# Attention steps that load their inputs first in a turn instead of last, with the squares at the turn's end

## The chip, the cores and the metric

One core of a Trainium2 chip runs the whole program. Its engines are PE (TensorE, matmuls), DVE (VectorE), ACT (ScalarE), POOL (GpSimd) and SP (SyncE, which here only issues DMAs, one after the other in program order). The metric is the device time of one execution in microseconds; lower is better. The kernel before takes 2015.22 us as the median of three runs.

## What is computed

The reference cut to what matters: an attention with random features, a mixture of eight experts on its result, and a second feed-forward stage.

```
q_s, k_s = (q * scale, k * scale)                 # (4, 8, 576, 64)
def phi(x):
    proj = einsum('bhsd,md->bhsm', x, omega)      # 128 features
    sq = sum(x * x, axis=-1, keepdims=True) / 2.0
    h = proj - sq
    h = h - max(h, axis=-1, keepdims=True)
    return exp(h) / sqrt(m)
q_p, k_p = (phi(q_s), phi(k_s))
kv = einsum('bhsm,bhsd->bhmd', k_p, v)
z = sum(k_p, axis=2)
num / den = q_p against kv and z
...
for e in range(E): out += P[:, e:e+1] * (maximum(x @ w1[e], 0.0) @ w2[e])
...
h = maximum(maximum(x @ w1, x @ w2), x @ w3);  return h @ w_out
```

The change touches the attention alone: the row sums of squares (`sq`), and the order of the loads around them.

## The kernel before

The attention has 16 steps, one for each batch and pair of heads. A step's keys and queries come as two tiles: `raw` (features on the partitions, for the matmuls; three buffers) and `sq` (tokens on the partitions, for the row sums of squares; two buffers), 576 KB each, loaded by SP in `load`. POOL squares `sq` in place (`squares`), DVE sums it to `bias` (`norms`), PE projects `raw` with `om` in three portions of 4, 4 and 1 token tiles (`A`), DVE takes the maxima of each portion and turns sums and maxima into a bias, and ACT makes the exponentials (`exps`, "E" in the list), `kp` for the first portion, `qp` for the second, `rem` for the last. `KV`, `QT`, `num` ("N") and `X` of earlier steps fill the rest: the products with the values, the transposes of `qp`, the quotient (ending in `xs`), and the transpose of the quotient into `xf`.

The program is a loop over turns from -2 on. The list `ORDER` says in which order a turn's pieces are written: `("A", 0, 0, 4)` is piece A of the step that belongs to this turn, a lag of -1 means the next turn's step, -2 the one after it. The instructions of each engine run in exactly this written order. `J` takes one job from a list that is there from time to time: in turns 5 to 13 the splits of finished `xf` blocks into `xh`, `xl` and differences `t` on POOL, and from turn 13 on the preparation of the first expert weights (`s`, `wh`, `wl` out of the loaded `st`), whose first four jobs are DVE additions. `G` is the expert logits, in turns 6, 10, 14 and 18 only.

From step 8 on (second half of the tokens) `X` also writes its block to DRAM: a DMA `x_of<-xf` on SP's queue that waits for ACT's copy in that turn, one for each of X's two parts. These turns are 10 and later. In turn 13 the first weight load `st` follows the second of these. Feed-forward layers begin in turn 16, and then take the rest of the span.

The first two steps are loaded ahead of the loop (`START`), and step 0's squares are made in two portions there.

Of the kernel before, what the change touches and what calls it, by code (L numbers as in the profile page):

```python
# [43 lines left out]
}  # L44

ORDER = [
# [3 lines left out]
]  # L50


# [1 line left out]
def tile_performer__moe__max3(ctx, tc, kq_t, kq, v1, omega2, w_gate, w1, w2, m1, m2, m3, m_out, out):  # L54
# [12 lines left out]
    N, DM = out.shape  # L67
    S = N // B
    E, _, FF = w1.shape
# [6 lines left out]
    G = HALF // S  # L76
# [33 lines left out]
    def tt(on, out, in0, in1, op):  # L110
        (nc.gpsimd if on == "P" else nc.vector).tensor_tensor(out=out, in0=in0, in1=in1, op=op)  # L111
# [457 lines left out]
    def attention(pool, proj_pool):  # L569
# [36 lines left out]
        def parts(s):  # L606
            return (slice(0, 4), slice(4, TP)) if s == 0 else (slice(0, TP),)
# [26 lines left out]
        def norms(s, part=None):  # L634

            if not part:
                bias[s] = proj_pool.tile([P, 2, TP, 2], F32, tag="bias", name="bias", bufs=2)
            bt = bias[s]
            for t in parts(s) if part is None else parts(s)[part : part + 1]:
                n = sq[s][:, t]  # L640
                if s == 0:
                    nc.scalar.square(n, n) if t.start else tt("P", n, n, n, ALU.mult)
                nc.vector.tensor_reduce(out=bt[:, 0, t], in_=n, axis=AX.X, op=ALU.add)
# [175 lines left out]
        def job():  # L819
            while todo:  # L820
# [4 lines left out]
                j()  # L825
                return True

        stages = dict(
            load=load, v=load_v, squares=squares, norms=norms,
            A=A, E=exps, KV=KV, QT=QT, N=num, X=X, G=logits,  # L830
        )
        early = {("squares", 0)}
# [3 lines left out]
        for turn in range(-2, NS + 3):  # L836
# [5 lines left out]
            for f, lag, *more in ORDER:  # L842
                s = turn - lag
# [44 lines left out]
    with tc.manual_schedule():  # L888
        make_identity(nc, ident)

        left = tc.tile_pool(name="att", bufs=1, side="left")
        right = tc.tile_pool(name="proj", bufs=1, side="right")
        with left as att:
            with right as proj:
                steps = attention(att, proj)
                while next(steps) < B * HP:
                    pass
            pools["a"] = ctx.enter_context(tc.tile_pool(name="a", bufs=1, side="right"))
            wslot[1] = tuple(pools["a"].tile([P, 7, 2, P], F32R, name=f"w{c}1") for c in "hl")
            load_ahead(2)  # L900
            layers = feed_forward()
            for n, _ in enumerate(steps):
                if n < FILL:
                    next(layers)
        smalls.clear()
        pools["b"] = ctx.enter_context(tc.tile_pool(name="b", bufs=1, side="left"))
        acc = big.tile([P, HT, DM], F32, tag="acc", name="acc")
        extra = gate()
        for n, _ in enumerate(layers):
            if n % 3 == 0:  # L910
                next(extra, None)
# [56 lines left out]
```

## Time and profile before

| | before |
|---|---|
| median of three runs | 2015.22 us (2014.66 to 2016.46) |
| the profiled execution | 2013.28 us, of it the span 2011.5 us |
| PE busy | 1955.9 us, 97% of the span |
| DVE, ACT, POOL busy | 1412.2, 805.9, 719.8 us |
| chain that ended last, by engine | PE 90%, DVE 5%, ACT 2%, DMA 1% |
| one line of that chain | DMA sq<-in_kq_dram 1% |

The busy shares are averages over a span of which the attention's turns 0 to 15 take the first 160 us or so. The chain of waits is followed back from the last instruction; a DMA in it is a transfer for which everything that came after it had to wait.

### The profile page before, as it was taken

The numbers are of one execution on the slowest core, as the hardware profiler recorded it, in microseconds if no ns is written. First come the engines' busy times: TensorE is split into PE (matmuls) and PEld (weight loads), VectorE is DVE, ScalarE is ACT, GpSimd is POOL, SyncE is SP. The second block draws the span as 40 slices with busy tenths as digits, with TensorE's granted clock in tenths as the row PEclk, the third lists the DMA queues.
The fourth block names the chain that finished last, engine by engine and source line by source line (L and its number), as shares of the span: only waits on it lengthen the run. The fifth ranks groups of instructions, "written<-read, shape, count | busy, mean of one in ns | idle before, by whom it ended". The sixth has DMA issues, their size and how long they took to land.

```text
span 2011.5 us, 33572 instructions
## 1 busy us (share of the span) xinstructions
PE 1955.9 (97%) x12906; PEld 1757.2 (87%) x12906; DVE 1412.2 (70%) x2735; ACT 805.9 (40%) x2011; POOL 719.8 (36%) x583
## 2 busy tenths in 40 slices
PE   7979999999999999999999999999999998998999
PEld 6868888998999889988899998999999897997898
DVE  6855778788878887768666666666666668658755
ACT  6865333333333333335333333333333334443442
POOL 3742234444443444324332222333322224333530
PEclk9989999999999999999999999999999999999999
DMA  6452112222222222223111111111111122212201
GB/s 207 166 162 77 43 48 74 91 84 84 74 74 74 74 79 94 63 74 93 62 47 49 43 43 43 43 43 53 52 44 43 43 66 71 85 43 90 90 22 48
DMA packets 93921, 143.42 MB, mean 71 GB/s; under 512 B 6848, under 2 KB 49984, under 8 KB 93760
## 3 DMA queue, kind: packets, MB, share of 16 engines
q1 hardware_dynamic: 93760, 141.28, 21.6%
q8 instruction: 101, 1.65, 0.3%
q14 instruction: 60, 0.49, 0.1%
HBM read 123.17 MB, written 18.09 MB: 70 GB/s over the span
## 4 chain that ended last, share of the span: by engine, by line
PE 90%; DVE 5%; ACT 2%; DMA 1%; issue 1%; POOL 0%; SPq 0%; DVEq 0%; ACTq 0%; POOLq 0%
PE ph L116 15%; PE ph L117 14%; PE ph L118 14%; PE po L394 9%; PE po L393 9%; PE po L395 9%; PE small L394 5%; PE small L393 5%; PE small L395 5%; PE ph L663 1%; PE ph L597 1%; DMA sq<-in_kq_dram 1%; DVE s L111 1%; DVE xl L111 1%; ACT qp L686 1%
## 5 line engine op out<-in xcount | busy, mean ns | idle before, releaser
L116 PE MATMUL ph<-xh,wh 128*128 128x288 f32 x2296 | 686.2, 299 | 17.1 <-ACT u L375 6.1
L117 PE MATMUL ph<-xl,wh 128*128 128x288 f32 x2296 | 681.3, 297 | 3.5 <-DVE xl L111 3.5
L118 PE MATMUL ph<-xh,wl 128*128 128x288 f32 x2296 | 677.6, 295 | 0.0
L116 PEld LDWEIGHTS ph<-xh,wh 128*128 128x128 f32 x2296 | 432.7, 188 | 51.1 <-ACT u L375 9.6
L117 PEld LDWEIGHTS ph<-xl,wh 128*128 128x128 f32 x2296 | 433.3, 189 | 29.2 <-DVE xl L111 4.2
L118 PEld LDWEIGHTS ph<-xh,wl 128*128 128x128 f32 x2296 | 434.2, 189 | 0.0
L411 DVE SCALAR_TENSOR_TENSOR acc<-po,prob,acc 128x512 f32<-128x512 f32 x354 | 265.3, 749 | 239.0 <-PE po L395 237.2
L111 POOL TENSOR_TENSOR w2l<-st,w2h 128x512 fp32r<-128x512 f32 x140 | 185.7, 1349 | 626.8 <-ACT w2h L108 600.8
L337 ACT ACTIVATE h<-ph 128x288 fp32r<-128x288 f32 x384 | 157.9, 412 | 451.4 <-DVE ph L111 402.0
L394 PE MATMUL po<-w2l,h 128*128 128x512 f32 x836 | 330.5, 395 | 0.0
L395 PE MATMUL po<-w2h,h 128*128 128x512 f32 x836 | 329.1, 394 | 0.4 <-DVE h L346 0.4
L393 PE MATMUL po<-w2h,h 128*128 128x512 f32 x836 | 329.5, 394 | 0.0
L111 POOL TENSOR_TENSOR wl<-st,wh 128x512 fp32r<-128x512 f32 (+1 forms) x162 | 169.4, 1052 | 281.6 <-ACT wh L108 280.4
L111 POOL TENSOR_TENSOR wl<-s,wh 128x512 fp32r<-128x512 f32 x162 | 214.6, 1329 | 33.1 <-ACT wh L108 29.7
L411 DVE SCALAR_TENSOR_TENSOR acc<-small,prob,acc 128x512 f32<-128x512 f32 x177 | 132.3, 748 | 84.9 <-PE small L395 84.6
L395 PEld LDWEIGHTS po<-w2h,h 128*128 128x128 f32 x836 | 157.7, 189 | 36.9 <-DVE h L346 0.8
L111 DVE TENSOR_TENSOR ph<-ph,u 128x288 f32<-128x288 f32 x304 | 140.1, 461 | 67.1 <-PE ph L118 53.8
L393 PEld LDWEIGHTS po<-w2h,h 128*128 128x128 f32 x836 | 157.7, 189 | 19.2
L394 PEld LDWEIGHTS po<-w2l,h 128*128 128x128 f32 x836 | 157.7, 189 | 18.4
L338 DVE SCALAR_TENSOR_TENSOR h<-ph,h 128x288 fp32r<-128x288 f32 x384 | 171.4, 447 | 1.2 <-ACT h L337 0.6
L394 PE MATMUL small<-w2l,h 128*128 128x512 f32 x424 | 167.2, 394 | 0.0
L395 PE MATMUL small<-w2h,h 128*128 128x512 f32 x424 | 166.3, 392 | 0.2 <-DVE h L346 0.2
(165 smaller groups left out, 2444.0 us busy)
## 6 DMA issues: line engine op xcount, KB each, us to landing
st<-in_moe_w_dram SPq DMA_DIRECT2D x146, 512.0 KB, 3.7
st<-plain SPq DMA_DIRECT2D x24, 512.0 KB, 3.7
raw<-in_kq_t_dram SPq DMA_DIRECT2D x15, 576.0 KB, 4.8
sq<-in_kq_dram SPq DMA_DIRECT2D x15, 576.0 KB, 6.0
plain<-d SPq DMA_DIRECT2D x24, 256.0 KB, 2.3
x_of<-xt SPq DMA_DIRECT2D x18, 256.0 KB, 2.7
out_dram<-acc SPq DMA_DIRECT2D x18, 256.0 KB, 2.0
v<-in_v_dram SPq DMA_DIRECT2D x16, 260.0 KB, 2.8
```

What stands on the lines that cost most here:

```text
L111: (nc.gpsimd if on == "P" else nc.vector).tensor_tensor(out=out, in0=in0, in1=in1, op=op)
L116: nc.tensor.matmul(ps, wh, xh, start=start and not onto, stop=False, **given)
L117: nc.tensor.matmul(ps, wh, xl, start=False, stop=False, **given)
L118: nc.tensor.matmul(ps, wl, xh, start=False, stop=stop, **given)
L337: after(0, lambda: nc.scalar.activation(hh, c, AF.Relu))
L338: after(1, lambda: nc.vector.scalar_tensor_tensor(out=hl, in0=c, scalar=0.0, in1=hh.bitcast(F32), op0=ALU.max, op1=ALU.subtract))
L393: nc.tensor.matmul(ps, h[:, f, ts], wh[:, f], start=f == 0, stop=False)
L394: nc.tensor.matmul(ps, h[:, f, ts], wl[:, f], start=False, stop=False)
L395: nc.tensor.matmul(ps, h[:, 2 + f, ts], wh[:, f], start=False, stop=f == 1)
L411: nc.vector.scalar_tensor_tensor(out=a, in0=ps, scalar=prob[:, i, e : e + 1], in1=a, op0=ALU.mult, op1=ALU.add)
L597: nc.tensor.matmul(o[j], w[:, j], x, start=start, stop=stop)
L663: nc.tensor.matmul(ps[h][:, i], x[d, t0 + i], om[d, h * M : (h + 1) * M], start=True, stop=True)
```

## The change

The load of the step two turns ahead moves from near the end of a turn to its very start. The squares move from the start of the turn before their step to the end of the turn two before it, behind N and ahead of the last J. The sum of squares (`norms`) stays where it is, right behind the first E, for all steps but step 1: that step's sum moves from the middle of turn 0 to its end (`late`).

```
 ORDER = [
-    ("squares", -1), ("A", 0, 0, 4), ("QT", 1, 0), ("X", 2, 1), ("QT", 1, 2), ("QT", 1, 1), ("G", 3), ("E", 0, 0, 4),
+    ("load", -2), ("A", 0, 0, 4), ("QT", 1, 0), ("X", 2, 1), ("QT", 1, 2), ("QT", 1, 1), ("G", 3), ("E", 0, 0, 4),
     ("v", 0), ("norms", -1), ("J", 0), ("A", 0, 4, 4), ("KV", 1), ("J", 0), ("X", 2, 0), ("E", 0, 4, 4),
-    ("A", 0, 8, 1), ("E", 0, 8, 1), ("N", 1), ("load", -2), ("J", 0),
+    ("A", 0, 8, 1), ("E", 0, 8, 1), ("N", 1), ("late", -1),
+    ("squares", -2), ("J", 0),
 ]
...
-            load=load, v=load_v, squares=squares, norms=norms,
+            load=load, v=load_v, squares=squares,
+            norms=lambda s, *part: s == 1 or norms(s, *part), late=lambda s: s == 1 and norms(s),
```

PE and ACT have the same rows in the same order in both kernels. Three engines' orders change.

On SP, around turns 9 to 11 before the change (`raw_1533`, `sq_1534` are step 11, `raw_1708`, `sq_1709` step 12, `v1_122` and `v0_121` the values of steps 9, 10 and 11 in turn):

```order
L624 DMA v1_122<-in_v1_dram 128x520
L625 DMA v1_122<-in_v1_dram 64x130
L613 DMA raw_1533<-in_kq_t_dram 128x1152
L614 DMA sq_1534<-in_kq_dram 128x1152
L764 DMA x_of1_96<-xf11_120 128x64
L624 DMA v0_121<-in_v1_dram 128x520
L625 DMA v0_121<-in_v1_dram 64x130
L764 DMA x_of1_96<-xf10_119 128x512
L613 DMA raw_1708<-in_kq_t_dram 128x1152
L614 DMA sq_1709<-in_kq_dram 128x1152
```

The same place after it (`raw_1392` and `sq_1393` are step 11, `raw_1540` and `sq_1541` step 12, `raw_1715` and `sq_1716` step 13):

```order
L614 DMA raw_1392<-in_kq_t_dram 128x1152
L615 DMA sq_1393<-in_kq_dram 128x1152
L625 DMA v1_122<-in_v1_dram 128x520
L626 DMA v1_122<-in_v1_dram 64x130
L614 DMA raw_1540<-in_kq_t_dram 128x1152
L615 DMA sq_1541<-in_kq_dram 128x1152
L765 DMA x_of1_96<-xf11_120 128x64
L625 DMA v0_121<-in_v1_dram 128x520
L626 DMA v0_121<-in_v1_dram 64x130
L765 DMA x_of1_96<-xf10_119 128x512
L614 DMA raw_1715<-in_kq_t_dram 128x1152
L615 DMA sq_1716<-in_kq_dram 128x1152
```

Step 12's two loads stood behind both DRAM writes of turn 10, and now stand ahead of them; step 13's stand behind them, where step 12's were.

On DVE, turn 0 before the change, from the bias of its first portion on (`bias<-sq 128x18` is the sum of squares of step 1, the reductions out of `po` and `ph` with 128x4 are the maxima, those with 128x2 the maxima of the last token tile):

```order
L680 SCALAR_TENSOR_TENSOR bias<-bias,small 128x8
L643 TENSOR_REDUCE bias<-sq 128x18
L666 TENSOR_REDUCE small<-po 128x4
L666 TENSOR_REDUCE small<-ph 128x4
L677 SCALAR_TENSOR_TENSOR small<-bias,small 128x8
L680 SCALAR_TENSOR_TENSOR bias<-bias,small 128x8
L657 TENSOR_REDUCE small<-ph 128x2
L677 SCALAR_TENSOR_TENSOR small<-bias,small 128x2
L680 SCALAR_TENSOR_TENSOR bias<-bias,small 128x2
L838 MEMSET gate_w 128x128
```

And after it:

```order
L681 SCALAR_TENSOR_TENSOR bias<-bias,small 128x8
L667 TENSOR_REDUCE small<-po 128x4
L667 TENSOR_REDUCE small<-ph 128x4
L678 SCALAR_TENSOR_TENSOR small<-bias,small 128x8
L681 SCALAR_TENSOR_TENSOR bias<-bias,small 128x8
L658 TENSOR_REDUCE small<-ph 128x2
L678 SCALAR_TENSOR_TENSOR small<-bias,small 128x2
L681 SCALAR_TENSOR_TENSOR bias<-bias,small 128x2
L644 TENSOR_REDUCE bias<-sq 128x18
L841 MEMSET gate_w 128x128
```

The sum of step 1 has gone behind the rest of turn 0's work on DVE.

On POOL, among the split jobs of turns 7 and 8, before the change (`sq_1236` is step 9's, squared at the start of turn 8):

```order
L108 CAST xh03_74<-t3_1023 128x576
L111 TENSOR_TENSOR xl03_75<-t3_1023,xh03_74 128x576
L111 TENSOR_TENSOR t6_1239<-xf0_118,t4_1086 128x576
L111 TENSOR_TENSOR sq_1236<-sq_1236 128x1152
L108 CAST xh06_80<-t6_1239 128x576
```

And after it (`sq_1090` is the same step 9):

```order
L109 CAST xh03_74<-t3_1027 128x576
L112 TENSOR_TENSOR xl03_75<-t3_1027,xh03_74 128x576
L112 TENSOR_TENSOR sq_1090<-sq_1090 128x1152
L112 TENSOR_TENSOR t6_1240<-xf0_118,t4_1087 128x576
L109 CAST xh06_80<-t6_1240 128x576
```

On POOL a step's squares have moved ahead of a single job, the last one of the turn.

## Rows read from the trace of the kernel before

**Rows 1.** Windows over turns 6, 7, 8 and 11 to 14; columns as headed.
```profile
core 0: us, PE busy (x) PEld busy (x) DVE busy (x) ACT busy (x) POOL busy (x), PEclk, DMA share, GB/s
...
57.80:66.25 8.45, 8.45 (x160) 7.14 (x159) 6.84 (x21) 6.83 (x25) 6.75 (x6) 1.00 0.49 170
66.25:74.26 8.01, 7.99 (x129) 6.68 (x129) 6.92 (x26) 7.03 (x25) 7.40 (x7) 1.00 0.60 197
...
81.74:89.13 7.39, 7.39 (x126) 6.28 (x125) 6.69 (x21) 6.79 (x25) 5.98 (x6) 1.00 0.49 166
...
97.87:111.28 13.41, 8.88 (x128) 7.18 (x127) 7.58 (x29) 8.19 (x29) 7.40 (x6) 1.00 0.74 235
111.28:121.65 10.37, 9.25 (x126) 7.38 (x126) 7.03 (x22) 6.96 (x25) 7.63 (x7) 0.84 0.27 72
121.65:134.58 12.93, 8.03 (x125) 6.59 (x125) 6.58 (x22) 6.95 (x25) 4.11 (x3) 0.92 0.77 252
134.58:146.59 12.01, 10.64 (x158) 8.78 (x158) 7.58 (x22) 6.26 (x22) 2.11 (x1) 0.80 0.16 45
```
**Rows 2.** Chain that ended last, in order of time: start, us, what.
```profile
4.78 6.73 DMA sq<-in_kq_dram
11.58 2.12 POOL sq L111
...
97.70 5.89 DMA sq<-in_kq_dram
103.72 2.12 POOL sq L111
...
120.45 6.43 DMA sq<-in_kq_dram
```
**Rows 3.** Timeline of SP's queue: start, us, line, DMA.
```profile
33.12 0.38 SPq L614 DMA_DIRECT2D sq<-in_kq_dram  x1
...
96.80 0.34 SPq L764 DMA_DIRECT2D x_of<-xf  x1
...
97.70 1.37 SPq L614 DMA_DIRECT2D sq<-in_kq_dram  x1
...
128.46 0.34 SPq L764 DMA_DIRECT2D x_of<-xf  x1
128.84 0.43 SPq L183 DMA_DIRECT2D st<-in_moe_w_dram  x1
```
**Rows 4.** Timeline of DVE in turns 0 and 1 [idle before it and its releaser].
```profile
9.53 0.16 DVE L680 SCALAR_TENSOR_TENSOR bias<-bias,small 128x8 f32<-128x8 f32 x1
13.71 1.35 DVE L643 TENSOR_REDUCE bias<-sq 128x18 f32<-128x1152 f32 x1 [4.02 <-POOL sq L111]
14.98 0.69 DVE L666 TENSOR_REDUCE small<-po 128x4 f32<-128x512 f32 x1
...
17.91 1.50 DVE L666 TENSOR_REDUCE small<-ph 128x4 f32<-128x512 f32 x2
...
23.08 1.50 DVE L666 TENSOR_REDUCE small<-ph 128x4 f32<-128x512 f32 x2 [1.97 <-PE ph L663]
```
**Rows 5.** Timeline of POOL and PE in turns 0 and 1.
```profile
15.31 2.11 POOL L111 TENSOR_TENSOR sq<-sq 128x1152 f32<-128x1152 f32 x1 [1.63 <-DMA sq<-in_kq_dram]
...
20.97 2.08 PE L663 MATMUL ph<-om,raw 64*128 64x128 f32 x16
```
**Rows 6.** Timelines of DVE at turn 10's end and of PE at turn 11's.
```profile
98.21 0.94 DVE L746 TENSOR_TENSOR xs<-ph,rc 128x256 f32<-128x256 f32 x3
...
110.25 0.45 PE L733 MATMUL ph<-kvs,qpT 128*64 128x65 f32 x4 [3.36 <-ACT qp L686]
```
**Rows 7.** Window inside turn 15, columns as in rows 1.
```profile
153.30:159.60 6.30, 6.25 (x60) 5.27 (x60) 1.73 (x4) 1.00 (x3) 0.00 (x0) 0.50 0.01 3
```
**Rows 8.** Tiles st and s: DMA landing, and DVE additions (ns min/median/max).
```profile
DMA to landing us min/median/max: 4.0/4.3/4.8
...
L111 DVE TENSOR_TENSOR s<-st x164: 406/416/1661, 135.4 to 1965.4; 128x256 f32<-128x256 f32 x164
```

## The prediction

> **What bounds the kernel now.** The page first: PE is busy 97% of the span and holds 90% of the chain that ended last, so only PE time or PE idle time is worth anything. One line of the chain does not belong there: a DMA into `sq`, 1% of the span. The chain in order of time shows where it lies: at the start, and again at 97.70 and 120.45 [rows 2]. Each time it is a load of `sq`, then POOL's squares, then DVE. A window for each turn shows what that costs [rows 1]: turns 6 to 8 take 8.45, 8.01 and 7.39 us with PE busy throughout (turn 6 has the logits, turn 7 their transpose), but turns 11 to 14 take 13.41, 10.37, 12.93 and 12.01. Turns 11 and 13 hold PE idle, 4.5 and 4.9 us. Turn 12 has only 1.1 us idle, but the granted clock is 0.84 on average, and in turn 14 it is 0.80.
>
> SP's queue shows why this begins at turn 11. Until turn 9 SP runs ahead of the other engines: step 5's `sq`, squared by POOL for turn 4, is issued at 33.12, in turn 2 [rows 3]. In turn 10 the queue holds a DRAM write that waits for ACT's copy of that same turn, at 96.80, and only behind it, at 97.70, `sq` of step 12 [rows 3]. Turn 11 begins at 97.87 [rows 1]. POOL gets its squares done at 105.8 and DVE, in order, takes its maxima of the second portion only behind their sum. PE then waits 3.36 us for ACT's `qp` exponentials [rows 6]. Turn 13 repeats it. Turn 12 escapes, because turn 11's stall gave its load time.
>
> **The change part by part.** It adds no instruction. On PE and ACT nothing moves.
>
> *Loads, turns 10 on.* Step 12's load now stands ahead of both writes of turn 10, step 13's where step 12's stood. A load is therefore issued about when the turn begins in whose end POOL squares it, and is summed in the middle of the next turn. Landing took 5.89 us and the squares 2.12 [rows 2], so the squares are done some 7.8 us after a turn's start; the sum comes at least a whole turn, 7.39, and the first portion's maxima, 1.50 [rows 4], later than that start, 8.9. Cover: 1.1 us at the least. The stalls of turns 11 and 13 go, and with them what follows an idle PE: in 153.30:159.60, after such an idle stretch, the granted clock is 0.50, the 1.2 GHz level, with PE busy 6.25 of 6.30 us [rows 7]; turns 12 and 14 lose by the same. I size the turns by undisturbed ones of rows 1:
> - turn 11 as turn 7 with a slightly longer transpose, 8.3: gains 5.1
> - turns 12 and 13 as turn 8, 7.39 put up to 7.45: gain 2.9 and 5.5
> - turn 14 as turn 6, 8.45, but see the next part.
>
> *What is late next: the first weights.* In turn 13 the `st` load is issued right behind the second DRAM write, 0.38 us after it [rows 3], and lands 4.3 us later [rows 8]: 4.7 after the write. The turn's last J, the addition `s` on DVE, needs it. In turn 10 DVE ended its quotients at 99.15 [rows 6], 2.35 us after the write at 96.80. In turn 13 before the change DVE was held up so long that `st` was there. Now DVE should wait 2.3 us, and behind it in its queue stand turn 14's maxima, for which ACT and so PE wait. DVE is busy 6.6 to 7.6 us in a turn of 7.4 to 8.5 [rows 1], so it has little to catch up with, and I let it count in full: turn 14 takes 8.45 + 2.3 = 10.75 and gains 1.3. Bounds: nothing of the 2.3 passes on (gain 3.6), or all of it does and the clock falls again (below).
>
> *Step 1's sum.* In turn 0 DVE stands still for 4.02 us before this sum [rows 4], for POOL squares only at 11.58 what landed then [rows 2]. Behind it wait the maxima of the second portion at 14.98. They now follow the bias that ends at 9.69, 5.3 us earlier; all of turn 0's DVE work then ends near 12.6. The sum itself stays at 13.71 to 15.06, and the maxima of turn 1, at 17.91 before, start at about 15.2. Turn 1's own sum, of step 2, waits for POOL, which squares it at 15.31 to 17.42 [rows 5], as early as before because its buffer is still freed at the same time; it ends at 18.8. PE's 16 projections at 20.97 [rows 5] waited, through ACT, for the bias behind the late maxima; 5 us earlier they run from 16.0 to 18.05. So the maxima at 23.08 [rows 4] start at 18.8, behind step 2's sum: **4.3 us**, and from there all is in the old order. Bounds: 2.3 where PE's matmuls do not reach their faster pace earlier too (those at 20.97 take 2.08 us for 16, and what PE does from 23 to 26 us would then cost some 2 us more), 5.3 where nothing holds back.
>
> *Squares.* The same instruction, 2.11 us [rows 5], one job earlier on POOL. Turns 2 to 9: loads are issued no earlier, since the `raw` buffer is freed by the projections of the turn before, and there PE had no wait to lose: 0. POOL is busy 6 to 7.6 us a turn [rows 1], so it keeps pace. The `v` loads, now behind a load each, still have a whole turn.
>
> A rule of the Trainium skill speaks against squares beside DVE additions. In rows 8 the addition `s<-st` takes 416 ns as a rule and up to 1661. The page "SBUF — State Buffer", section "Who interferes with whom", says that a DVE instruction with two SBUF inputs and a GpSimd instruction that reads SBUF exclude each other for a whole instruction. The spread of rows 8 is what this would look like; by it, `s` in turn 13 could meet step 15's squares and the sum would be 1.2 us (1661 against 416 ns) smaller. I count nothing: by the times above the squares end about 8 us into turn 13, and `st` lands near 11.
>
> Sum: 4.3 + 5.1 + 2.9 + 5.5 + 1.3 = **19.1 us**. The profiled execution, 2013.28 us with its span of 2011.5, would go to 1994.2; it lies 1.9 below the median of the runs, so by the median 2015.22 - 19.1 = **1996.1**. The rest of the span starts that much earlier and is bound by PE alone.
>
> **The rivals.**
> - *The clock falls in turn 14.* The new wait leaves PE idle about 2 us. Against: turn 12's 1.1 us of idle are not what began its low clock, that came from turn 11. For: 3.36 us were enough [rows 6]. Price: as turn 14 lost before; a mean of 0.80 over 12.01 us [rows 1] is 4.8 us at 0.50, of which half is lost, 2.4: 1998.5.
> - *Better than summed.* `st` lands early enough for the DVE, and turn 15, for which I changed nothing, keeps its clock: 6.25 busy us at half pace [rows 7] become 3.1. 1996.1 - 2.3 - 3.1 = 1990.7.
> - *The wait moves to POOL.* If landings take the 6.73 of rows 2 and a split job or two of the turn before still stand ahead, the cover of 1.1 us is gone; at 2 us in each of turns 11 to 13 the time is 2002. For: POOL is busy 7.40 to 7.63 us in turns 11 and 12, as long as an undisturbed turn.
> - *The port rule bites:* `s` meets the squares, 1.2 us: 1997.3.
> - *It doesn't do what it says from turn 10 on*, because a buffer and not the DRAM write holds the loads: only the start, 2010.9. Against: the write at 96.80 and the load right behind it [rows 3].
> - *Slower.* `v` now stands behind 1152 KB of loads in SP's queue. It has a whole turn, 7.4 us; landings reach 6.73 [rows 2]. If it lands later than that, KV holds PE in each of 14 turns: from 1.4 us late in each, a landing of 8.8 us, all 19.1 are lost, and at 2 us late the time is 2024. `v` is less than half as large as a load, so it should not be slower than one.
>
> **How the numbers follow.** The forecast as summed 0.45, from 1993 to 1998 by its bounds; clock in turn 14 0.20; better 0.14; POOL 0.10; port rule 0.04; start alone 0.05; slower 0.02. The likeliest is 1996.1. A range of 1990 to 2003.5 reaches from the better case to the POOL case with the lower bound of the start, and leaves out the last two and a little of each tail, under 2 in 10. A change of 0.2%, 4 us, is about what a measurement can tell: all cases but the last two are faster by more, and start alone lies at that border. Faster 0.93, same 0.05, slower 0.02.
>
> **What would show it.** Right: the second kind of chain link, DMA into `sq`, gone after the start; `sq` of step 12 issued ahead of both DRAM writes of turn 10, a turn earlier than now; turns 11 to 13 near 7.4 to 8.3 us at a granted clock of 1.00; DVE's sum in turn 0 behind the maxima, and turn 2 some 4 us earlier; a wait of DVE's `s` for the DMA into `st` of about 2 us at the end of turn 13. Wrong: POOL waiting for `sq` with a sum behind it, PE waiting for `v`, or a turn 12 or 13 above 9 us.

## The result, and the profile after

The changed kernel takes **1998.47 us** (median of four runs, 1995.05 to 2001.0) against 2014.94 for the kernel before (2013.86 to 2016.46): ratio 0.9917, 95% interval 0.9899 to 0.9935, 16.5 us less. The forecast was 1996.1. The profiled execution took 2000.06 us with a span of 1998.3, 13.2 less than before's, where the sum of the prediction asked for 19.1.

The first part of the page after, with the busy time of each engine, and its chain by engine:

```profile
PE 1951.9 (98%) x12906; PEld 1753.4 (88%) x12906; DVE 1411.7 (71%) x2735; ACT 806.7 (40%) x2011; POOL 719.5 (36%) x583
...
PE 90%; DVE 5%; ACT 3%; issue 1%; DMA 1%; POOL 0%; SPq 0%; DVEq 0%; ACTq 0%
```

PE was busy for 4 us less than before; the rest of the 13.2 us came out of its waits. The chain in order of time, as in [rows 2]:

```profile
4.78 6.74 DMA sq<-in_kq_dram
11.59 2.12 POOL sq L112
...
119.77 4.43 DMA st<-in_moe_w_dram
```

The load and the squares at the start are there as before. The two loads of `sq` at 97.70 and 120.45 have gone; in their place stands one load, of the first weights `st`, near the end of turn 13. SP's queue, as in [rows 3]:

```profile
83.87 0.38 SPq L615 DMA_DIRECT2D sq<-in_kq_dram  x1
87.25 0.33 SPq L765 DMA_DIRECT2D x_of<-xf  x1
...
92.31 0.34 SPq L765 DMA_DIRECT2D x_of<-xf  x1
...
93.22 1.99 SPq L615 DMA_DIRECT2D sq<-in_kq_dram  x1
...
119.40 0.33 SPq L765 DMA_DIRECT2D x_of<-xf  x1
119.77 0.44 SPq L184 DMA_DIRECT2D st<-in_moe_w_dram  x1
```

Step 12's load now stands ahead of both DRAM writes of turn 10, not behind them: 83.87 instead of 97.70. Windows for turns 11 to 15 (columns as in [rows 1]; a turn begins with the first projection of its step, and turn 15 ends where PE begins to transpose its `qp`):

```profile
93.39:103.66 10.27, 8.89 (x129) 7.19 (x128) 7.60 (x29) 8.12 (x29) 6.91 (x6) 1.00 0.69 201
103.66:112.58 8.92, 7.78 (x126) 6.39 (x126) 6.93 (x22) 6.87 (x25) 6.89 (x6) 1.00 0.68 203
112.58:121.50 8.92, 7.78 (x125) 6.39 (x125) 6.84 (x22) 6.88 (x25) 4.76 (x4) 1.00 0.60 198
121.50:133.91 12.41, 10.04 (x157) 8.29 (x157) 7.17 (x20) 6.82 (x24) 0.00 (x0) 0.86 0.28 86
133.91:148.38 14.47, 11.48 (x128) 9.37 (x126) 6.61 (x28) 9.17 (x31) 4.41 (x4) 0.76 0.38 115
```

Turns 11 to 13 have lost their long stall and run at a granted clock of 1.00, but they are not the 8.3 and 7.45 us that were forecast: 10.27, 8.92 and 8.92, each with over 1 us of PE idle. Turn 14 is longer than before (12.41 against 12.01), at a clock of 0.86. DVE in turns 0 and 1, as in [rows 4], and at the end of turn 13 (in brackets the idle time before an instruction and what ended it):

```profile
9.54 0.17 DVE L681 SCALAR_TENSOR_TENSOR bias<-bias,small 128x8 f32<-128x8 f32 x1
9.80 0.70 DVE L667 TENSOR_REDUCE small<-po 128x4 f32<-128x512 f32 x1
...
13.73 1.35 DVE L644 TENSOR_REDUCE bias<-sq 128x18 f32<-128x1152 f32 x1 [1.09 <-POOL sq L112]
15.14 1.44 DVE L667 TENSOR_REDUCE small<-ph 128x4 f32<-128x512 f32 x2
...
17.47 1.35 DVE L644 TENSOR_REDUCE bias<-sq 128x18 f32<-128x1152 f32 x1 [0.49 <-POOL sq L112]
...
124.22 0.43 DVE L112 TENSOR_TENSOR s<-st 128x256 f32<-128x256 f32 x1 [2.06 <-DMA st<-in_moe_w_dram]
```

The maxima that stood behind step 1's sum at 14.98 are at 9.80, those of turn 1 at 15.14 instead of 17.91. Turn 2 begins at 20.72 instead of 26.37, and turn 3, which is past the sums that still hold turn 2, at 29.71 instead of 34.22.

### The profile page after: what moved, and what is told of

It is laid out like the page before. It is cut to its first block, busy times and chain, and to the rows that moved or that the text cites. A ratio compares the mean times of both kernels' runs of the same rounds, so it can differ in the third digit from the quotient of the medians.

```text
span 1998.3 us, 33551 instructions
## 1 busy us (share of the span) xinstructions
PE 1951.9 (98%) x12906; PEld 1753.4 (88%) x12906; DVE 1411.7 (71%) x2735; ACT 806.7 (40%) x2011; POOL 719.5 (36%) x583
## 4 chain that ended last, share of the span: by engine, by line
PE 90%; DVE 5%; ACT 3%; issue 1%; DMA 1%; POOL 0%; SPq 0%; DVEq 0%; ACTq 0%
PE ph L117 14%; PE ph L118 14%; PE ph L119 14%; PE po L395 9%; PE po L394 9%; PE po L396 9%; PE small L395 5%; PE small L394 5%; PE small L396 5%; PE ph L664 1%; PE ph L598 1%; DVE s L112 1%; DVE xl L112 1%; ACT qp L687 1%; DVE t L112 1%
## 5 line engine op out<-in xcount | busy, mean ns | idle before, releaser
L394 PEld LDWEIGHTS po<-w2h,h 128*128 128x128 f32 x836 | 157.7, 189 | 19.1
```

The source lines that it names most:

```text
L394: nc.tensor.matmul(ps, h[:, f, ts], wh[:, f], start=f == 0, stop=False)
```

## The experiments

Seven kernels, all timed in five rounds. The first four ran together, beside a median of 2013.59 for the kernel before, the other three together, beside 2013.9.

**1. The sum alone.** The kernel before, and of the change only step 1's sum at the end of turn 0.

```
-    ("A", 0, 8, 1), ("E", 0, 8, 1), ("N", 1), ("load", -2), ("J", 0),
+    ("A", 0, 8, 1), ("E", 0, 8, 1), ("N", 1), ("late", -1), ("load", -2), ("J", 0),
```

> Before, with step 1's sum alone moved to the end of turn 0; loads and squares stay where they were. If the start and the loads are two separate gains, this gives the 4.3 us of the forecast (the trace of the changed kernel shows 4.5 at turn 3): about 2010.6, with the stalls of turns 11 and 13 as before. Rival, the start's gain is given back at the first load stall because that load then has less time: 2014 to 2015.

Measured: 2009.59 us (2006.17 to 2011.9), ratio 0.998 [0.9971, 0.9989], 4.0 us faster. Turn 3 begins at 29.77, as after the whole change. Turns 11 and 13 of this kernel, in windows:

```profile
93.45:107.09 13.64, 8.89 (x129) 7.18 (x128) 7.59 (x29) 8.22 (x29) 7.42 (x6) 1.00 0.73 231
...
117.50:130.03 12.53, 8.04 (x125) 6.59 (x125) 6.59 (x22) 6.98 (x25) 4.11 (x3) 0.90 0.73 241
```

The stalls are still there in full. So the term of the start stands by itself, and the rest of the gain is not the sum's.

**2. The load alone.** The kernel before with the load first in a turn; squares at the start of the next turn and step 1's sum as before.

```
-    ("squares", -1), ("A", 0, 0, 4), ("QT", 1, 0), ...
+    ("load", -2), ("squares", -1), ("A", 0, 0, 4), ("QT", 1, 0), ...
...
-    ("A", 0, 8, 1), ("E", 0, 8, 1), ("N", 1), ("load", -2), ("J", 0),
+    ("A", 0, 8, 1), ("E", 0, 8, 1), ("N", 1), ("J", 0),
```

> Before, with the load alone moved to the front of a turn; squares stay at the start of the next turn and step 1's sum in the middle of turn 0. My theory: the loads are the whole of the second gain, so turns 11 to 13 take what they take in the changed kernel (10.3, 8.9, 8.9 us against 13.4, 10.4, 12.9) and the total is 9 to 12 us below before, about 2004. Rival, the squares had to move too: POOL still waits with them at a turn's start, sums are late, and turns 11 to 13 stay above 10.5 us each.

Measured: 2004.12 us (2002.42 to 2005.71), ratio 0.9946 [0.9934, 0.9959]. Its turns 11 and 12:

```profile
98.74:108.99 10.25, 8.88 (x128) 7.18 (x127) 7.59 (x29) 8.09 (x29) 6.61 (x6) 1.00 0.70 201
108.99:117.90 8.91, 7.78 (x125) 6.39 (x126) 6.94 (x22) 6.86 (x25) 7.47 (x7) 1.00 0.68 206
```

These are the lengths of the whole change, to 0.02 us, so the earlier load alone takes the stalls away. It also shows that the residue of 1 to 2 us a turn has nothing to do with the squares.

**3. Without the late sum.** The changed kernel with step 1's sum back in the middle of turn 0.

```
-            norms=lambda s, *part: s == 1 or norms(s, *part), late=lambda s: s == 1 and norms(s),
+            norms=norms, late=lambda s: None,
```

> The changed kernel with step 1's sum put back into the middle of turn 0, so loads and squares moved only. If the squares' place is worth nothing, this equals the run with the load alone, about 2004, and lies 4.3 us above the changed kernel. If squares being earlier matters, it lies below the run with the load alone by 1 us or more per turn from 11 to 13.

Measured: 2003.47 us (2000.34 to 2007.79), ratio 0.9947 [0.9935, 0.9959], the same as the load alone; turns 11 and 12 take 10.25 and 8.91. Where the squares stand is worth nothing that can be measured. In kernels 2 and 3 turn 2 begins 0.9 and 1.75 us later than before the change. The windows from the second portion of turn 1 to the start of turn 2 (before, kernel 2, kernel 3) show why:

```profile
20.97:26.37 5.40, 5.40 (x95) 4.71 (x94) 2.81 (x10) 4.27 (x16) 2.11 (x1) 1.00 0.58 215
20.71:27.25 6.54, 6.54 (x96) 5.78 (x95) 2.82 (x10) 4.71 (x18) 2.11 (x1) 0.63 0.41 142
21.82:28.12 6.30, 6.30 (x96) 5.58 (x95) 2.81 (x10) 4.48 (x17) 2.11 (x1) 0.66 0.45 157
```

PE is busy throughout in all three with the same work, and the granted clock is lower in kernels 2 and 3 (the projections at 20.97 take 2.08 us before the change too, [rows 5], so its 1.00 is too high for their part); kernel 3 also enters the stretch 0.85 us later. Why the clock rises later there was not settled.

**4. The first weights earlier.** The changed kernel with the load of `st` behind the first DRAM write of turn 13, not the second.

```
+            if part == 1 and hp == HP - 1 and b == G:
+                load_ahead(1)
             if part == 0:
...
-                        load_ahead(1)
```

> The changed kernel with the first weight load issued behind the first DRAM write of turn 13, not the second, some 4 us earlier. The wait of DVE's first addition for it (2.06 us in the changed kernel) goes. My theory: turn 14 shortens by about that, from 12.4 to near 10, and PE idles less in front of KV, so its lower clock in turn 14 may go as well, 1 us more: 1994 to 1996. Rival, DVE's wait was covered or turn 15 gives it back: 1998 as the changed kernel.

Measured: 1997.36 us (1995.88 to 1998.53), ratio 0.9914 [0.9902, 0.9927], against 0.9917 for the change alone: no difference that can be told. Yet its turn 14 is this (window, then SP's and DVE's timelines):

```profile
121.57:131.44 9.87, 8.50 (x157) 7.12 (x157) 7.24 (x20) 6.16 (x22) 0.00 (x0) 1.00 0.16 45
...
115.61 0.67 SPq L184 DMA_DIRECT2D st<-in_moe_w_dram  x1
...
122.17 0.41 DVE L112 TENSOR_TENSOR s<-st 128x256 f32<-128x256 f32 x1
```

The load is issued 4.2 us earlier, DVE no longer waits for it, and turn 14 goes from 12.41 us at 0.86 to 9.87 at 1.00. This shows the price of the new wait: 2.54 us, of which 1.54 are PE's busy time (10.04 to 8.50, the half-pace part) and 1.0 is idle. Turn 15 takes 14.08 us against 14.47, so the attention ends 2.9 us earlier in this trace (145.52 against 148.38). Of that only 1.6 is left in the span (1996.7): some 1.6 us are lost in one place far behind the attention, where the clock falls in this trace and not in the changed kernel's (last section), and smaller differences elsewhere make up the rest. So the median of four runs does not resolve what the trace shows. In turn 15 PE stands still again:

```profile
137.18 0.48 PE L664 MATMUL po<-om,raw 64*128 64x128 f32 x2 [1.80 <-ACT kp L687]
```

**5. Banks in step.** What makes turns 11 to 13 longer than turns 7 to 9? Grouping the instructions of PE in turn 12 of the changed kernel shows the only idle time of weight in front of projections:

```profile
L664 PE MATMUL ph<-om,raw 64*128 64x128 f32 x25 | 2.7, 288 | 1.2 <-ACT qp L687 1.2
```

A projection needs `raw` and `om` and nothing of `qp`. What ACT's `qp` exponentials do hold is a PSUM bank: `abank()` hands seven banks out by a rotating list of buffer names (five called `ph`, two `po`). A plain turn takes 14, two whole rounds, so a piece meets the same place of the list in every turn. The logits of turns 6, 10 and 14 take one more, and their transpose another in the turn behind, so that from turn 11 on all pieces are two places further on than in turns 7 to 9, and, by the theory, a projection gets a bank that ACT reads late. The names show the shift: turn 12's first projections go to `ph` and `po` alternately, those of turns 7 to 9 to `ph` alone. Which buffer of a name a piece gets, the profile does not show. The experiment hands out five unused banks ahead of turn 10's logits, so that turns 11 to 13 meet the list as turns 7 to 9 did; no instruction is added on PE, DVE or ACT.

```
+            if b in (1,):
+                kept = outs[0]
+                for _ in range(5):
+                    abank()
+                outs[0] = kept
             ps = abank()
```

> The changed kernel with five PSUM banks taken and left unused ahead of turn 10's logits, so that the round of seven banks stands in turns 11 to 13 as it stood in turns 7 to 9. My theory of the missing part of the gain: turns 11 to 13 take 10.3, 8.9 and 8.9 us not for any load but because the logits have shifted which bank a projection must wait for; then they go to about 7.6, 7.9 and 7.5 and the total falls by about 5, to 1993. Rival, they are long because of ACT's and SP's own work in these turns (the DRAM writes): they stay at 10.3, 8.9, 8.9 and the total at 1998.

Measured: 1991.89 us (1986.8 to 1994.22), ratio 0.9889 [0.9875, 0.9903]. Turns 11 to 15, and the same group of projections in turn 12:

```profile
93.62:101.30 7.68, 7.68 (x129) 6.57 (x128) 6.82 (x24) 6.86 (x24) 4.24 (x4) 1.00 0.77 233
101.30:108.96 7.66, 7.66 (x128) 6.55 (x126) 6.85 (x23) 7.06 (x26) 7.27 (x6) 1.00 0.76 237
108.96:116.52 7.56, 7.56 (x128) 6.45 (x126) 6.75 (x22) 6.95 (x26) 6.83 (x6) 1.00 0.76 237
116.52:127.89 11.37, 8.60 (x159) 7.15 (x158) 7.87 (x29) 7.26 (x26) 0.00 (x0) 0.96 0.39 120
127.89:141.20 13.31, 12.53 (x126) 10.56 (x126) 6.40 (x25) 10.04 (x33) 4.41 (x4) 0.65 0.37 122
...
L664 PE MATMUL ph<-om,raw 64*128 64x128 f32 x33 | 2.9, 288 | 0.0
```

Turns 11 to 13 fall from 28.1 to 22.9 us together, PE is busy throughout, and the wait for `qp` is gone. That shows the banks, as nothing else was changed. Turn 14 still has the wait for `st`, 2.97 us on DVE here, and the granted clock of turn 15 is 0.65.

**6. Both.** Experiments 4 and 5 together, with five unused banks ahead of turn 14's logits too (`b in (1, 2)`), so that turn 15 meets the list as turn 7 does. This third edit was not timed by itself.

> The changed kernel with the early weight load and the unused banks ahead of the logits of turns 10 and 14. If the two are separate: 2.5 us in turn 14 and 5 in turns 11 to 13 together, turn 15 begins near 126 us and the total is about 1992. Rival, turn 15 or the feed-forward's start gives a part back, as with the early weights alone, where turn 14 gained 2.5 and the span 1.6: 1994 to 1995.

Measured: **1984.9 us** (1982.94 to 1985.34), ratio 0.9858 [0.9844, 0.9871], the fastest kernel of the study and 7 us better than experiment 5. Turns 14 and 15, and the projections that waited 1.80 us in experiment 4:

```profile
116.61:125.08 8.47, 8.47 (x160) 7.16 (x158) 7.66 (x25) 7.23 (x26) 1.02 (x1) 1.00 0.27 81
125.08:133.73 8.65, 8.11 (x128) 6.74 (x126) 5.94 (x23) 8.50 (x29) 4.43 (x4) 1.00 0.60 191
...
128.29 0.48 PE L664 MATMUL ph<-om,raw 64*128 64x128 f32 x2 [0.31 <-DVE prob L819]
```

Turn 14 is 8.47 us, what the prediction gave it without a wait (8.45). The clock stays at 1.00 through turn 15, which takes 8.65 us instead of 14.47. The total is 7 us below the 1992 that was expected for two separate repairs, and the rival missed by more. The span behind turn 15's start is 8.3 us shorter than that of the changed kernel (1981.2 - 125.08 = 1856.1 against 1998.3 - 133.91 = 1864.4). Of this 5.8 are turn 15; the other 2.5 lie behind the attention, where low clock falls in different places in the two traces, and are not shown to come from the edit. Experiments 4 and 5 each leave a stall of PE in turn 14 or 15 and a lower clock in turn 15 (14.08 us at 0.88, 13.31 at 0.65); the three edits together keep the clock. Whether turn 15 owes that to `st` in time or to its own banks was not separated.

**7. Weight preparation spread out.** In experiment 6 ACT is busy for nearly all of turn 15 (8.50 of 8.65 us), and ahead of its exponentials of that turn stand four copies of weights, some 2 us, as all weight jobs are written at once ahead of that turn. Here they are spread over turn 15 in its `J` places, the rest ahead of turn 16.

```
-            while turn == NS - 1 and job():
+            if turn == NS - 1:
+                load_ahead(2)
+            while turn == NS and job():
...
-                    if turn < NS - 1:
+                    if turn < NS:
```

> As the run before, and the preparation of the first weights no longer all at the start of turn 15 but one job at each of its three places, the rest at the start of turn 16. In turn 15 PE stands still about 2 us behind ACT's exponentials, which stand behind four copies of weights, and then runs 6 us at half clock. If the copies are the cause, turn 15 shortens from 14 us to 10 or 11 and the total is 2 to 4 us below the run before, about 1989. Rival, the feed-forward's first products then wait for the weights: no gain, or up to 3 us more.

Measured: 1986.64 us (1985.69 to 1988.8), ratio 0.987 [0.9856, 0.9883], 1.7 us more than experiment 6, with no overlap of the runs. Turn 15, and PE's first feed-forward products, which now wait for the weights:

```profile
124.64:132.35 7.71, 7.64 (x128) 6.46 (x127) 5.98 (x23) 7.20 (x25) 1.46 (x2) 1.00 0.66 205
...
134.93 0.40 PE L117 MATMUL ph<-xh,wh 128*128 128x288 f32 x1 [0.72 <-ACT wh L109]
...
136.28 0.40 PE L119 MATMUL ph<-xh,wl 128*128 128x288 f32 x1 [0.82 <-POOL wl L112]
```

Turn 15 did shorten, by 0.9 us (7.71 against 8.65), but the waits of 0.72 and 0.82 us behind it, and a stretch at a lower granted clock after them (0.94 from 132.35 to 160 us), cost more. The rival of the expectation held.

## Why the prediction was right, and where it was not

The direction, the mechanism and the range held: 1998.47 lies in 1990 to 2003.5, 2.4 us from the forecast. The sizes held less well, and part of that nearness is luck. The parts, in the profiled executions:

| term | predicted | measured |
|---|---|---|
| step 1's sum, to turn 3 | 4.3 | 4.5 |
| turn 11 | 5.1 | 3.1 |
| turn 12 | 2.9 | 1.5 |
| turn 13 | 5.5 | 4.0 |
| turn 14 | 1.3 | -0.4 |
| sum | 19.1 | 12.7 (span 13.2) |

- **Step 1's sum** went as worked out: the rows at 9.80, 13.73 and 15.14 stand where the prediction put them, and experiment 1 gives 4.0 us by itself. Turn 2 even begins 5.65 us earlier and hands 1.1 back by turn 3, as turn 1's second maxima wait behind step 2's sum, which ends at 18.8 as forecast, and ACT and PE wait for them in turn 2.
- **The loads from turn 10 on** were the right mechanism, shown from both sides: without the load's move the stalls stay (experiment 1), with it alone they go (experiment 2).
- **The size of turns 11 to 13** is the step that failed most: "I size the turns by undisturbed ones of rows 1". They gained 8.6 us together, not 13.5. The turns taken as a measure differ from turns 11 to 13 in more than the stall, namely in the phase of the seven PSUM banks; experiment 5 put the phase right and got 7.68, 7.66 and 7.56. The row for it was there: turn 12 of [rows 1], without a stall of its own, has 1.1 us of PE idle, and the prediction blamed the whole of its 10.37 us on what turn 11 left behind. Of its 2.9 us only 1.5, the clock, could go. Beside it the prediction's windows of [rows 1] were misread: the second starts at turn 7 but runs half a us into turn 8, and the third, called turn 8, is turn 9. Turns 7, 8 and 9 before the change:

```profile
66.18:73.75 7.57, 7.57 (x129) 6.46 (x127) 6.50 (x20) 6.59 (x23) 7.01 (x6) 1.00 0.61 201
73.75:81.67 7.92, 7.90 (x127) 6.59 (x125) 7.00 (x25) 7.32 (x27) 7.28 (x6) 1.00 0.52 183
81.67:89.13 7.46, 7.46 (x127) 6.35 (x125) 6.75 (x22) 6.86 (x25) 6.05 (x6) 1.00 0.48 165
```

  So turn 11 was sized too long and turn 12 too short; the three together, 22.95 us, come within 0.3 of the 23.2 that the prediction used, and of the 22.9 of experiment 5.
- **The new wait for `st`** came as described: 2.06 us on DVE, forecast 2.3. **Turn 14** has one term more than forecast: 8.47 undisturbed, 1.40 for the banks (experiment 4 against 6) and 2.54 for the wait with its clock (change against experiment 4), together 12.41; forecast were 8.45 + 2.3. The split depends on the order of the repairs: experiment 5, banks first, took turn 14 to 11.37 only. Not all of the wait was passed on, as PE idle grew by 1.0 us, but the clock fell too, to 0.86. That is the rival "the clock falls in turn 14", priced at 2.4 beyond a full wait; the wait and the clock together cost hardly more than the wait alone was meant to. That the rival's 1998.5 is the measured time is a coincidence: most of what was missing is in turns 11 to 13.
- **The other rivals.** The wait did not move to POOL: squares of turn 11 waited 3.21 us for their load and held nobody, since their sum is half a turn away. `s` took 0.43 us, so there was no meeting with the squares. Elsewhere in the changed kernel's trace such meetings are to be seen: of the 164 additions `s<-st`, the 22 that took over 0.6 us all overlap an instruction on POOL, and none that meets no POOL instruction takes over 0.43. The longest on DVE, and what POOL does meanwhile:

```profile
1846.69 1.66 DVE L112 TENSOR_TENSOR s<-st 128x256 f32<-128x256 f32 x1
...
1846.63 3.02 POOL L112 TENSOR_TENSOR xl<-h,xh 128x576 fp32r<-128x576 f32 x2 [7.42 <-ACT xh L109]
```

  The Trainium skill's page "SBUF — State Buffer", section "Who interferes with whom", says that a DVE instruction with two SBUF inputs contends with a POOL instruction that reads SBUF, and these rows agree with it. `v` never held PE, though it is 292 KB, a little over half of a 576 KB load and not under, as the prediction had it. "Better than summed" did not happen to the change, but experiment 6 has it: `st` in time and a turn 15 at full clock, with the banks in step besides.

The profiled executions gained 13.2 us, 0.5 of it in turn 15 (14.99 to 14.47 us), for which nothing was forecast; the medians differ by 16.5. The profiled execution is 1.6 us above the median of its kernel, and that of before 1.7 below. The interval of the ratio reaches from 13.1 to 20.4 us, so four runs of each tell neither 13.2 from 16.5 nor 16.5 from the forecast's 19.1, and a hit to 2.4 us says little for the sizes: in the traces turns 11 to 14 gained 6.6 us less than forecast. Runs of one kernel spread by 6 us, and the faster ones tend to have the higher granted clock (experiment 1: 2006.17 us at a mean of 0.994, 2011.9 at 0.989).

## What to carry to other kernels

When loads and writes that wait for computation share an in-order queue, put the load ahead of the write; the load's place was worth 9.5 us here, and the place of the squares nothing that could be measured. Size a repaired stretch by one that is like it in everything: what a rotation of buffers hands out depends on how many were taken before, and one extra buffer far upstream changes every turn behind it. Look for the next late thing, and repair a chain of stalls to its end: in the traces the attention ended 2.9 us earlier with the weights alone, 7.2 with the banks alone and 14.65 with both and turn 14's banks, and most of the surplus over the sum is turn 15 at full clock.

## What was not expected of the hardware

The rotation of PSUM buffers alone made the same turns 7.68, 7.66 and 7.56 us, or 10.27, 8.92 and 8.92. The granted clock stayed at 1.00 in turns 11 to 13 of the changed kernel, with 1.1 to 1.4 us of idle in pieces of 0.6 us and less, but fell in turn 14 with 2.37 us in one piece, whose row is this:

```profile
128.73 0.69 PE L598 MATMUL po<-v,kp 128*64 128x65 f32 x16 [2.37 <-ACT kp L687]
```

In experiment 4 the same place had 1.37 us of idle, and the clock of turn 14 stayed at 1.00; the 1.80 us in its turn 15, shown there, stand ahead of a window (137 to 146 us) at 0.81.

The length of a single wait does not decide it alone. In the feed-forward stage PE waits about 2.5 us for DVE at the same place in each kernel; here the wait and the 10 us behind it, first in the changed kernel, then in experiment 4:

```profile
205.15 0.40 PE L117 MATMUL ph<-xh,wh 128*128 128x288 f32 x1 [2.48 <-DVE c L112]
205.15:215.15 10.00, 10.00 (x61) 9.14 (x62) 8.68 (x25) 3.68 (x9) 3.47 (x3) 1.00 0.18 55
...
202.88 0.40 PE L117 MATMUL ph<-xh,wh 128*128 128x288 f32 x1 [2.48 <-DVE c L112]
202.88:212.88 10.00, 10.00 (x51) 8.98 (x52) 6.79 (x18) 3.67 (x9) 3.44 (x3) 0.83 0.20 55
```

The same wait left the clock at 1.00 once and was followed by 0.83 the other time, with 51 matmuls done in the 10 us instead of 61. What decides is open.
